# A branch-free tail for the last four experts, one width for the large product, fixed buffers, and logits as column tiles

## The chip, the cores and the metric

The kernel runs on one core of a Trainium2 chip. The metric is the device time of one execution in microseconds, and shorter is better. The core has five engines with a queue of instructions each, which run beside one another and wait for one another by semaphores: PE (matrix products, with PEld as its loading of the stationary operand), DVE and ACT (element-wise work), POOL (element-wise work, and here the indirect transfers) and SP (which only issues transfers). PE writes its results into eight banks of accumulation memory.

## The reference

Three stages follow one another. Block-causal attention gives 1152 token vectors of 512 numbers. A gated product `(x @ w_a) * (x @ w_b) @ w_out` with 1536 inner columns follows (its weights are 64-bit floats). Then each token goes to one of 8 experts:

```python
logits = x @ w_gate                       # 1152 x 8
expert_idx = np.argmax(logits, axis=1)
gate_w = softmax(logits)[np.arange(N), expert_idx]
for i in range(N):                        # capacity = 288 rows per expert
    e = expert_idx[i]
    if counts[e] < capacity:
        disp[e, counts[e]] = x[i]
        pos[i] = counts[e]; counts[e] += 1; keep[i] = True
h = np.maximum(np.einsum('ecd,edf->ecf', disp, w1), 0.0)   # 512 -> 1024
y = np.einsum('ecf,efd->ecd', h, w2)                       # 1024 -> 512
out[i] = gate_w[i] * y[expert_idx[i], pos[i]] if keep[i] else 0
```

How many tokens an expert gets is known only on the chip. With the data drawn here the eight experts get 0, 217, 640 (cut to 288), 274, 3, 2, 2 and 14 tokens.

## The kernel before

**Attention and gated product.** A hand-written order of steps interleaves attention, the decoding of the 64-bit weights, and the first products. Products that must be exact are made of three passes of a faster number format: each operand is split into a high and a low part (`hi`, `lo`), and PE runs hi by hi, hi by lo and lo by hi. This part is untouched but for the buffer of `w_gate`.

**Token stage.** For each of the nine tiles of 128 tokens, PE makes the second product of the gated stage (`y_part`, 36 matmuls, L567). Between pieces of it the steps of the tile before are placed: `y_turn` transposes its 512 columns, `logits` (L589) multiplies with `w_gate`, giving 8 rows by 128 tokens summed over four slices `kd` in one accumulation, ACT copies them, `choose` (L596) transposes them back and DVE finds the maximum and the expert, and `place` (L619) counts positions by a product with a triangle and scatters each token's row into the buffer `xdisp` in device memory by an indirect transfer of POOL (L637). After the last tile the counts of all experts (`cnt`) are known.

**Experts.** The counts are loaded into registers of all five engines (`load_count`, L710). An expert with more than 64 tokens takes the large path: `wide` (L822) computes the first product of all its rows in eight pieces `f`, 12 matmuls each, for 256 or for 288 rows (two forms behind one branch); `blocks` (L854) computes the second product in blocks of 128, 128 and 32 rows, each followed by `put`, an indirect transfer of the rows to the output (L797). An expert with 1 to 64 tokens takes the small path: `few_first` (L878) multiplies 64 rows with the plain 32-bit weights, in two halves that share one bank, with two weight chunks on two halves of PE's columns; `few_turn` transposes, `few_second` (L896) is the second product. An expert with none does nothing. Ahead of each expert's second product stands the preparation of the next one: `x_turn` transposes its rows on PE (L781, three blocks, each in a bank of its own out of a pool of three) and splits them into hi and lo on ACT and DVE (L784, L785), and `split_first` splits its first weights (L744 on ACT, L745 on DVE: two chunks in four pieces). The second weights are split inside `wide`, one piece at every other `f`.

Every one of these is inside a branch on a register that PE, ACT, DVE and POOL take together:

```python
with most(e, HB) as big:
    ...
    x_turn(e + 1)
    split_first(e + 1)
    blocks(e, 0)
with big.Else():
    with least(e) as some:
        few_first(e)
```

The weights come from device memory in chunks of 1 MB (`wraw`, four to an expert, L548), into a pool of nine buffers. Nine are asked for at the start of the token stage, and after each expert SP asks for the next four, as buffers come free. The rows of an expert are read back from `xdisp` by `xload` (L732 to L736).

Of the kernel before, what the change touches and what calls it, by code (L numbers as in the profile page):

```python
# [11 lines left out]
F32 = mybir.dt.float32  # L12
# [14 lines left out]
G = 32  # L27
# [39 lines left out]
def fused_kernel(ctx: ExitStack, tc, q, k, v, w_a, w_b, w_out, w_gate, w1, w2, consts, out, cap):  # L67
# [376 lines left out]
    wg_sb = gp.tile([P, KD, E], F32, name="wg_sb")  # L444
    nc.sync.dma_start(out=wg_sb, in_=w_gate.rearrange("(k p) e -> p k e", p=P))
# [85 lines left out]
    NW = 9  # L531
    wr_pool = es_r.enter_context(tc.tile_pool(name="wr_pool", bufs=NW, side="right"))
# [3 lines left out]
    chunks = [(e, w, c) for e in range(E) for w, n_ in ((0, CPE), (1, KC)) for c in range(n_)]  # L536
    raws = {}

    def fetch_to(m):

        for n in range(len(raws), min(m, len(chunks))):
            e, which, c = chunks[n]
            raw = wr_pool.tile([P, KD, HALF], F32, tag="wraw", name=f"wraw{n}")
# [7 lines left out]
    fetch_to(NW)  # L551
# [33 lines left out]
    def logits(t):  # L585
        s = tok[t]
        plt_ = psG.tile([P, P], F32, tag="plt", name=f"plt{t}")
        for kd in range(KD):
            nc.tensor.matmul(plt_[:E], lhsT=wg_sb[:, kd], rhs=s["yT"][:, kd], start=(kd == 0), stop=(kd == KD - 1))  # L589
        s["lgT"] = sp.tile([E, P], F32, tag="lgT", name=f"lgT{t}")  # L590
        nc.scalar.copy(s["lgT"], plt_[:E])

    def choose(t):
        s = tok[t]
        plg = psG.tile([P, E], F32, tag="plg", name=f"plg{t}")
        nc.tensor.transpose(plg, s["lgT"], ident[:E, :E])  # L596
# [16 lines left out]
        s["oh"] = oh  # L613

    def place(t):
# [4 lines left out]
        nc.tensor.matmul(ppos, lhsT=ones, rhs=acc, start=False, stop=True)  # L620
        t2 = sp.tile([P, E], F32, tag="t2", name=f"t2{t}")
        nc.vector.tensor_tensor(out=t2, in0=ppos, in1=oh, op=ALU.mult)
        nc.vector.tensor_reduce(out=pos, in_=t2, op=ALU.add, axis=AX.X)
        slot = sp.tile([P, 2], F32, tag="slot", name=f"slot{t}")
        nc.vector.tensor_scalar(
            out=slot[:, 0:1], in0=pos, scalar1=float(cap), scalar2=float(FAR), op0=ALU.is_ge, op1=ALU.mult
        )
        nc.vector.scalar_tensor_tensor(
            out=slot[:, 1:2], in0=idx, scalar=float(cap), in1=pos, op0=ALU.mult, op1=ALU.add
        )  # L630
        sl_i = sp.tile([P, 1], I32, tag="sl", name=f"sl{t}")
        nc.vector.tensor_tensor(out=sl_i, in0=slot[:, 0:1], in1=slot[:, 1:2], op=ALU.add)
        nc.vector.tensor_tensor(out=acc, in0=acc, in1=oh, op=ALU.add)
        row = s["row"]
        nc.vector.tensor_scalar_add(sm, sm, 1e-9)
        nc.vector.reciprocal(row[:, DM:DM + 1], sm)
# [6 lines left out]
    for t in range(NT):  # L643
# [24 lines left out]
    few = keep.tile([P, E], F32, name="few")  # L668
    nc.vector.tensor_scalar(out=few, in0=pct, scalar1=float(P // 2), scalar2=-2.0, op0=ALU.is_le, op1=ALU.mult)
# [8 lines left out]
    psH = es_m.enter_context(tc.tile_pool(name="psH", bufs=3, space=PSUM))  # L678
    psT = es_m.enter_context(tc.tile_pool(name="psT", bufs=3, space=PSUM))
    psO = es_m.enter_context(tc.tile_pool(name="psO", bufs=2, space=PSUM))  # L680
# [18 lines left out]
    y_ = [[mp.tile([P, DM], F32, name=f"y{i}_{j}") for j in range(len(blks))] for i in range(2)]  # L699
# [6 lines left out]
    def load_count(e):  # L706
# [7 lines left out]
        hs = [h for g in engines[:4] for h in regs[e, g].val.handles]  # L714
        regs[e] = RuntimeValue.of_register_unchecked(RegisterHandles(hs))
# [9 lines left out]
    def xload(e):  # L725
        if e >= E:
            return
        st[e] = {"xd": []}
        for j, (r, m) in enumerate(blks):
            st[e]["xd"].append(mp.tile([P, ROW], F32, tag=f"xd{j}", name=f"xd{e}_{j}", bufs=3))  # L730
        xd = st[e]["xd"]
        nc.sync.dma_start(out=xd[0][:HB, :], in_=xdisp[e * cap:e * cap + HB, :])  # L732
        with most((e, ET.SP), HB):
            nc.sync.dma_start(out=xd[0][HB:P, :], in_=xdisp[e * cap + HB:e * cap + P, :])
            for j, (r, m) in enumerate(blks[1:], 1):
                nc.sync.dma_start(out=xd[j][:m, :], in_=xdisp[e * cap + r:e * cap + r + m, :])  # L736
# [240 lines left out]
```

## Time and profile before

| | |
|---|---|
| median of three runs | 531.5 us (527.62, 531.5, 532.93) |
| the profiled execution, own time | 535.47 us |
| its span, first to last instruction | 533.4 us |
| mean granted TensorE clock | 0.957 |
| PE busy | 477.7 us, 90% of the span |
| DVE, ACT, POOL busy | 48%, 35%, 24% |
| weight chunks `wraw` | 32 transfers of 1 MB, 10.6 us each from issue to landing (median) |

The profile is one execution. Its own time is 2.1 us over its span, and 4.0 us over the median of the runs. PE's busy time counts pipelined matmuls to their modelled ends, so it says where PE works, not that it works at its peak. [...]

### The profile page before, as it was taken

The numbers are of one execution on the slowest core, as the hardware profiler recorded it, in microseconds if no ns is written. First come the engines' busy times: TensorE is split into PE (matmuls) and PEld (weight loads), VectorE is DVE, ScalarE is ACT, GpSimd is POOL, SyncE is SP. The second block draws the span as 40 slices with busy tenths as digits, with TensorE's granted clock in tenths as the row PEclk, the third lists the DMA queues.
The fourth block names the chain that finished last, engine by engine and source line by source line (L and its number), as shares of the span: only waits on it lengthen the run. The fifth ranks groups of instructions, "written<-read, shape, count | busy, mean of one in ns | idle before, by whom it ended". The sixth has DMA issues, their size and how long they took to land. (4 is left out here: it accounts for less than half of the span.)

```text
span 533.4 us, 7946 instructions
## 1 busy us (share of the span) xinstructions
PE 477.7 (90%) x2808; PEld 379.3 (71%) x2808; DVE 255.1 (48%) x495; ACT 189.0 (35%) x391; POOL 126.8 (24%) x133
## 2 busy tenths in 40 slices
PE   6899999999999899999999999981898999966684
PEld 3465556779999899999977777761887968732241
DVE  2689996736464656473333343434472816010111
ACT  2577777523232324331422222213362615110111
POOL 1447767510413142330102010011101020011010
PEclk9899999999999999999999999996698999896979
DMA  7666310025455565650099010002846327079620
GB/s 166 150 188 173 85 23 2 1 81 179 161 178 177 171 209 180 211 177 1 1 349 378 22 41 20 21 4 68 265 147 237 126 93 280 23 268 328 217 106 4
DMA packets 67260, 73.48 MB, mean 138 GB/s; under 512 B 31395, under 2 KB 43811, under 8 KB 67185
## 3 DMA queue, kind: packets, MB, share of 16 engines
q1 hardware_dynamic: 64384, 68.80, 39.9%
q0 software_dynamic: 1456, 3.29, 1.6%
q8 instruction: 40, 0.66, 0.5%
q10 hardware_dynamic: 1344, 0.44, 0.3%
q14 instruction: 36, 0.29, 0.2%
HBM read 62.12 MB, written 11.72 MB: 138 GB/s over the span
## 5 line engine op out<-in xcount | busy, mean ns | idle before, releaser
L418 PE MATMUL p<-xTh,hi 128*128 128x384 f32 x272 | 91.4, 336 | 3.8 <-ACT asb L483 2.5
L418 PE MATMUL p<-xTh,lo 128*128 128x384 f32 x272 | 90.9, 334 | 0.0
L418 PE MATMUL p<-xTl,hi 128*128 128x384 f32 x272 | 90.9, 334 | 0.0
L278 POOL TENSOR_TENSOR PB<-PB,rs 128x576 f32<-128x576 f32 (+4 forms) x40 | 52.4, 1333 | 42.4 <-DVE rs L267 34.4
L418 PEld LDWEIGHTS p<-xTh,hi 128*128 128x128 f32 x272 | 51.0, 188 | 5.4 <-ACT asb L483 3.9
L418 PEld LDWEIGHTS p<-xTl,hi 128*128 128x128 f32 x272 | 51.1, 188 | 0.0
L418 PEld LDWEIGHTS p<-xTh,lo 128*128 128x128 f32 x272 | 51.1, 188 | 0.0
L822 PE MATMUL ph<-xt,whi 128*128 128x288 f32 (+1 forms) x192 | 41.5, 312 | 4.8 <-DMA xdisp<-row,sl 1.8
L567 PE MATMUL py<-woh,gh 128*128 128x512 f32 x108 | 45.7, 423 | 0.0
L567 PE MATMUL py<-woh,gl 128*128 128x512 f32 x108 | 42.7, 396 | 0.0
L567 PE MATMUL py<-wol,gh 128*128 128x512 f32 x108 | 42.5, 394 | 0.0
L797 POOL DMA_INDIRECT out<-y,ti x12 | 11.3, 945 | 120.1 <-ACT y L861 67.5
L253 ACT ACTIVATE PB<-sc,nm 128x256 f32<-128x256 f32 (+3 forms) x64 | 33.1, 531 | 16.8 <-DVE nm L242 11.4
L211 PE MATMUL sc<-k,q 64*64 64x288 f32 (+4 forms) x192 | 36.8, 493 | 2.2 <-ACT PB L258 1.1
L854 PE MATMUL po<-whi,ht 128*128 128x512 f32 (+1 forms) x112 | 37.9, 407 | 0.4 <-issue 0.4
L822 PEld LDWEIGHTS ph<-xt,whi 128*128 128x128 f32 x192 | 33.4, 207 | 5.5 <-issue 3.6
L381 POOL TENSOR_TENSOR wol<-wob,woh 128x1024 fp32r<-128x1024 f32 x6 | 14.5, 2422 | 92.4 <-ACT woh L380 78.8
L242 DVE TENSOR_REDUCE nm<-sc 128x2 f32<-128x512 f32 (+4 forms) x40 | 31.2, 802 | 8.4 <-PE sc L211 4.2
L408 POOL TENSOR_TENSOR lo<-bits,hi 128x1024 fp32r<-128x1024 f32 x12 | 28.7, 2391 | 24.7 <-ACT hi L402 24.7
L745 DVE TENSOR_TENSOR wlo<-wraw,whi 128x1024 fp32r<-128x1024 f32 x24 | 28.6, 1220 | 9.8 <-ACT whi L744 9.3
L878 PE MATMUL pf<-wraw,xs 128*64 128x256 f32 x128 | 19.7, 458 | 14.8 <-issue 7.5
L484 DVE TENSOR_TENSOR g_sb<-asb,p 128x384 f32<-128x384 f32 x34 | 18.3, 551 | 29.8 <-PE p L418 15.2
(129 smaller groups left out, 809.6 us busy)
## 6 DMA issues: line engine op xcount, KB each, us to landing
wraw<-in_moe_w SPq DMA_DIRECT2D x32, 1024.0 KB, 10.6
raw<-in_moe_w_a SPq DMA_DIRECT2D x12, 512.0 KB, 3.9
raw<-in_moe_w_b SPq DMA_DIRECT2D x12, 512.0 KB, 5.7
wor<-in_moe_w_out SPq DMA_DIRECT2D x6, 1024.0 KB, 6.7
xdisp<-zrow SPq DMA_DIRECT2D x6, 774.0 KB, 8.0
out<-zrow SPq DMA_DIRECT2D x3, 768.0 KB, 7.6
QK<-in_q SPq DMA_DIRECT2D x16, 128.0 KB, 2.9
V<-in_v SPq DMA_DIRECT2D x16, 128.0 KB, 2.6
```

The lines of the kernel that those rows point to most:

```text
L211: nc.tensor.matmul(dst, lhsT=qT[n][hs, P * i:min(P * i + P, S)], rhs=kT[n][hs, c0:c0 + cw], start=True, stop=(i == LAST), skip_group_check ...
L242: nc.vector.tensor_reduce(out=soft[n][0][:, c:c + cnt], in_=view, op=ALU.max, axis=AX.X if i < NQ else AX.XY, negate=True)
L253: nc.scalar.activation(out=dst[:, h], in_=view[:, h], func=AF.Exp, bias=nm[:, c + h:c + h + 1], accum_out=sm[:, c + h:c + h + 1],)
L278: nc.gpsimd.tensor_tensor(out=x, in0=x, in1=r, op=ALU.mult)
L408: nc.gpsimd.tensor_tensor(out=lo, in0=f32(m), in1=f32(hi), op=ALU.subtract)
L418: nc.tensor.matmul(ps, lhsT=lt, rhs=rt, start=(n_ == 0), stop=(n_ == len(seq) - 1))
L484: nc.vector.tensor_tensor(out=g_sb[:, f, c * CH:(c + 1) * CH], in0=asb, in1=pb, op=ALU.mult)
L567: nc.tensor.matmul(s["py"], lhsT=lt[:, f], rhs=rt[:, f], start=(f == 0 and i == 0), stop=(f == NF - 1 and i == 2))
L745: nc.vector.tensor_tensor(out=lo[:, a:a + 2], in0=raw[:, a:a + 2], in1=f32(hi[:, a:a + 2]), op=ALU.subtract)
L822: nc.tensor.matmul(ph[:, 0:n].rearrange("p (g c) -> p g c", c=G), lhsT=lt, rhs=rt, start=(n_ == 0), stop=(n_ == len(seq) - 1),)
L854: nc.tensor.matmul(po[:2 * m if tail else m], lhsT=lt, rhs=rt, start=(f == 0 and i == 0), stop=(f == KF2 - 1 and i == len(seq) - 1),)
L878: nc.tensor.matmul(ph[c * HB:(c + 1) * HB, cs], lhsT=s["xs"][:, kd], rhs=raws[e, 0, c][:, kd, cs], start=(kd == 0), stop=(kd == KD - 1), s ...
```

## The change

- **Tail.** DVE also computes `left`, the largest count of experts 4 to 7. After the first four experts all five engines load it and branch once: if it is over 64, experts 4 to 7 run as before, otherwise `run_few` runs the small path for all four with no further branch. In the small path the two halves of the first product use two banks, and consecutive experts use different ones.
- **One form.** `wide` always computes 288 rows.
- **Buffers.** Pools give way to fixed tiles: twelve weight chunks in place of nine (three are in room that is free only after the token stage), three pairs of hi and lo rooms in place of four, two sets of row buffers `xd` in place of three, one set of output rows `y` in place of two, four banks `pH` for the first product in place of three, two banks `pT` for transposes in place of three. With three rooms `split_first` splits one chunk (two pieces), and `wide` splits the other three, one piece after each of `f` 0 to 5. `split_first` now stands ahead of `x_turn`, and only ACT and DVE take its branch.
- **Start of the experts.** The rows of experts 0 and 1 are read in full without a branch, then chunks 9 to 11; the rows of expert 2 are read after expert 0.
- **Token stage.** `w_gate` is padded with zeros to 32 columns. Each of the four slices `kd` is a matmul of its own on its own 32 columns of PE, the full 128 by 128 result is transposed, and DVE adds the four parts. In `place` one of the DVE steps goes, two stand earlier, and the reciprocal is ahead of the slot.

```diff
-        for kd in range(KD):
-            nc.tensor.matmul(plt_[:E], lhsT=wg_sb[:, kd], rhs=s["yT"][:, kd], start=(kd == 0), stop=(kd == KD - 1))
+            nc.tensor.matmul(
+                plt_[kd * CT:(kd + 1) * CT], lhsT=wg_sb[:, kd], rhs=s["yT"][:, kd], start=True, stop=True,
+                skip_group_check=True, tile_position=(0, kd * CT),
+            )
...
-        nc.tensor.transpose(plg, s["lgT"], ident[:E, :E])
+        nc.tensor.transpose(pl4, s["lgT"], ident)
+        plg = sp.tile([P, E], F32, tag="lg", name=f"lg{t}")
+        nc.vector.tensor_reduce(
+            out=plg, in_=pl4.rearrange("p (k c) -> p c k", c=CT)[:, 0:E], op=ALU.add, axis=AX.X
+        )
...
+    nc.vector.tensor_reduce(out=left, in_=pct[:, E // 2:], op=ALU.max, axis=AX.X)
...
-    parts = {
-        (w, c): [hp.tile([P, KD, HALF], F32R, name=f"w{nm}{w}_{c}") for nm in ("hi", "lo")]
-        for w in range(2) for c in range(CPE)
-    }
+    rooms = [[hp.tile([P, KD, HALF], F32R, name=f"w{nm}{i}") for nm in ("hi", "lo")] for i in range(3)]
+
+    def parts(e, which, c):
+        return rooms[((2 * e + which) * CPE + c) % 3]
...
+    pH = [psM.tile([P, HALF], F32, name=f"pH{i}") for i in range(4)]
+    pT = [psM.tile([P, KD, P], F32, name=f"pT{i}") for i in range(2)]
+    pO = [psM.tile([P, DM], F32, name=f"pO{i}") for i in range(2)]
...
+    def xload_now(es):
...
+        for js in ((0,), range(1, len(blks))):
+            for e in es:
+                for j in js:
+                    r, m = blks[j]
+                    nc.sync.dma_start(out=xd_[e % 2][j][:m, :], in_=xdisp[e * cap + r:e * cap + r + m, :])
...
     def split_first(e):
         if e < E:
-            with most(e, HB):
-                for piece in halves(e, 0):
+            with most((e, "split"), HB):
+                for piece in halves(e, 0, 0):
                     piece()
...
+    def x_all(e):
+        s = st[e]
+        xd, xt = s["xd"], s["xt"]
+        for j, (r, m) in enumerate(blks):
+            pt = pT[j % 2]
+            for kd in range(KD):
+                nc.tensor.transpose(pt[:, kd, :m], xd[j][:m, kd * P:(kd + 1) * P], ident[:m, :m])
...
+            nc.scalar.copy(xh, src)
+            nc.vector.tensor_tensor(out=xl, in0=src, in1=f32(xh), op=ALU.subtract)
...
-        todo = halves(e, 1)
+        todo = halves(e, 0, 1) + halves(e, 1, 0) + halves(e, 1, 1)
...
-            if todo and f % 2 == 0:
+            if todo:
                 todo.pop(0)()
...
     def few_first(e):
-        ph = psH.tile([P, HALF], F32, tag="ph", name=f"pf{e}")
         for g in range(2):
+            ph = pH[e % 2 * 2 + g]
...
-            x_turn(e + 1)
             split_first(e + 1)
+            x_turn(e + 1)
             blocks(e, 0)
...
+    def run_few(e0):
+
+        for e in range(e0, E):
+            few_first(e)
+            few_turn(e, 0)
+            if e + 1 < E:
+                x_rooms(e + 1)
+                x_few(e + 1)
+            few_turn(e, 1)
+            few_second(e)
+            if e + 3 < E:
+                xload(e + 3, whole=False)
+            fetch_to(NW + 2 * CPE * (e + 1))
...
+    run(0, MID)
...
+    with tc.If(regs["left"] > HB) as many:
+        run(MID, E)
+    with many.Else():
...
+        run_few(MID)
```

The change moves instructions at three places. The first is PE at the end of expert 1's first product (`ph` before, `pH` now), where the rows of expert 2 are transposed; `px2_0` to `px2_2` are the three banks before, `pT0` and `pT1` the two banks now, and the waits of a row stand in brackets. Before:

```order
L822 MATMUL ph1_7_256_4343<-xt_3369,wlo0_1_3364 128x256
L908 UNCONDITIONAL_BRANCH
L777 COMPARE_AND_BRANCH
L781 MATMUL px2_0_4359<-cst_62,xd2_0_3454 128x128 [waits DMAHW3_49,DMAHW2_49]
L781 MATMUL px2_0_4359<-cst_62,xd2_0_3454 128x128 x3
L781 MATMUL px2_1_4368<-cst_62,xd2_1_3455 128x128 [waits DMAHW4_49]
L781 MATMUL px2_1_4368<-cst_62,xd2_1_3455 128x128 x3
L781 MATMUL px2_2_4377<-cst_62,xd2_2_3456 128x32 [waits DMAHW5_49]
L781 MATMUL px2_2_4377<-cst_62,xd2_2_3456 128x32 x3
L777 UNCONDITIONAL_BRANCH
```

Now:

```order
L865 MATMUL pH3_3424<-xt_3397,wlo2_3396 128x288
L784 UNCONDITIONAL_BRANCH
L828 COMPARE_AND_BRANCH
L809 MATMUL pT0_3425<-cst_62,xd0_0_3412 128x128 [waits DMAHW4_49,DMAHW3_49,DMAHW2_49]
L809 MATMUL pT0_3425<-cst_62,xd0_0_3412 128x128 x3
L809 MATMUL pT1_3426<-cst_62,xd0_1_3413 128x128 [waits DMAHW5_49]
L809 MATMUL pT1_3426<-cst_62,xd0_1_3413 128x128 x3
L809 MATMUL pT0_3425<-cst_62,xd0_2_3414 128x32 [waits DMAHW6_49,DVE_49]
L809 MATMUL pT0_3425<-cst_62,xd0_2_3414 128x32 x3
L828 UNCONDITIONAL_BRANCH
```

The third transpose now goes into the bank of the first one, and waits for DVE, which reads that bank; before it waited for its transfer alone.

The second place is DVE's queue at the same point, after the last piece of expert 1's first product. `xt` are the low parts of expert 2's rows, `wlo` the low parts of its first weights. Before:

```order
L777 COMPARE_AND_BRANCH
L785 TENSOR_TENSOR xt_3369<-px2_0_4359,xt_3369 128x4x4x32 [waits Activation_49]
L785 TENSOR_TENSOR xt_3369<-px2_1_4368,xt_3369 128x4x4x32 [waits Activation_49]
L785 TENSOR_TENSOR xt_3369<-px2_2_4377,xt_3369 128x4x32 [waits Activation_49]
L777 UNCONDITIONAL_BRANCH
L788 COMPARE_AND_BRANCH
L788 UNCONDITIONAL_BRANCH [waits DVE_49] x2
L753 COMPARE_AND_BRANCH
L745 TENSOR_TENSOR wlo0_0_3362<-wraw8_2542,whi0_0_3361 128x1024 [waits DMAHW1_49,Activation_49]
L745 TENSOR_TENSOR wlo0_0_3362<-wraw8_2542,whi0_0_3361 128x1024 [waits Activation_49]
L745 TENSOR_TENSOR wlo0_1_3364<-wraw9_4069,whi0_1_3363 128x1024 [waits DMAHW2_49,Activation_49]
L745 TENSOR_TENSOR wlo0_1_3364<-wraw9_4069,whi0_1_3363 128x1024 [waits Activation_49]
```

Now:

```order
L784 COMPARE_AND_BRANCH
L776 TENSOR_TENSOR wlo2_3396<-wraw8_2535,whi2_3395 128x1024 [waits DMAHW1_49,DVE_49,Activation_49]
L776 TENSOR_TENSOR wlo2_3396<-wraw8_2535,whi2_3395 128x1024 [waits DVE_49,Activation_49]
L784 UNCONDITIONAL_BRANCH
L784 UNCONDITIONAL_BRANCH [waits DVE_49]
L828 COMPARE_AND_BRANCH
L813 TENSOR_TENSOR xt_3397<-pT0_3425,xt_3397 128x4x4x32 [waits DVE_49,Activation_49]
L813 TENSOR_TENSOR xt_3397<-pT1_3426,xt_3397 128x4x4x32 [waits DVE_49,Activation_49]
L813 TENSOR_TENSOR xt_3397<-pT0_3425,xt_3397 128x4x32 [waits Activation_49]
L828 UNCONDITIONAL_BRANCH
```

The two weight pieces now stand ahead of the three row pieces, of which the first frees the bank that PE waits for; before, four weight pieces stood behind them. ACT's queue, which makes the high parts, has the same new order.

The third place is PE after the second product of expert 4 (`pq4` before, `pO0` now). Before:

```order
L896 MATMUL pq4_6257<-wraw18_5205,hf_3392 64x512
L896 MATMUL pq4_6257<-wraw19_5207,hf_3392 64x512
L753 COMPARE_AND_BRANCH
L753 UNCONDITIONAL_BRANCH x2
L753 COMPARE_AND_BRANCH
L753 UNCONDITIONAL_BRANCH x2
L777 COMPARE_AND_BRANCH
```

Now:

```order
L939 MATMUL pO0_3427<-wraw6_2533,hf_3431 64x512 [waits DVE_49]
L939 MATMUL pO0_3427<-wraw7_2534,hf_3431 64x512
L939 MATMUL pO0_3427<-wraw6_2533,hf_3431 64x512
L939 MATMUL pO0_3427<-wraw7_2534,hf_3431 64x512
L921 MATMUL pH2_3423<-wraw8_2535,xs1_3399 64x256 [waits DMAHW3_49,Activation_49]
L921 MATMUL pH2_3423<-wraw9_3388,xs1_3399 64x256 [waits DMASW4_49,DMASW5_49,DMASW3_49,DMASW6_49,DMASW2_49,DMASW7_49,DMASW1_49,DMAHW4_49,DMASW0_49,Pool_49]
```

Behind the second product there were branches over the other paths, the first part of expert 5 some 240 rows further on; now expert 5's first product (`pH2`) is the next row.

## Rows read from the trace of the kernel before

**Rows 1.** Windows by stage: PE, PEld, DVE, ACT, POOL busy, granted clock, DMA, GB/s

```profile
265.00:358.00 93.00, 92.87 (x448) 69.01 (x446) 34.96 (x121) 20.71 (x40) 10.15 (x15) 1.00 0.32 120
...
403.80:436.50 32.70, 30.89 (x172) 26.74 (x172) 14.64 (x27) 14.12 (x22) 3.95 (x10) 0.95 0.45 157
...
469.70:533.40 63.70, 40.74 (x220) 18.75 (x220) 7.10 (x13) 7.59 (x16) 5.99 (x14) 0.86 0.54 189
```

**Rows 2.** Timeline of PE, one token tile: start, duration, instruction, shape, count

```profile
340.19 0.39 PE L567 MATMUL py<-wol,gh 128*128 128x512 f32 x1
340.42 0.40 PE L567 MATMUL py<-woh,gl 128*128 128x512 f32 x1
340.75 1.04 PE L589 MATMUL plt<-yT,wg_sb 128*8 128x128 f32 x8
341.72 0.50 PE L567 MATMUL py<-woh,gh 128*128 128x512 f32 x1
...
344.01 0.22 PE L596 MATMUL plg<-cst,lgT 8*128 8x8 f32 x1
```

**Rows 3.** Timeline between token stage and first expert; idle time before in brackets

```profile
365.25 0.98 POOL L637 DMA_INDIRECT xdisp<-row,sl  x1 [4.91 <-DVE cnt L670]
...
369.16 0.87 SPq L734 DMA_DIRECT2D xd<-xdisp  x1
...
372.77 2.55 PE L781 MATMUL px<-cst,xd 128*128 128x128 f32 x12 [8.48 <-DVE wlo L745]
...
376.62 0.76 PE L822 MATMUL ph<-xt,whi 128*128 128x256 f32 x2 [1.29 <-POOL gate L773]
```

**Rows 4.** Chain of waits: expert 3's first product

```profile
438.09 13.03 PE ph L822 x95
```

**Rows 5.** Expert 2 to 3: chain of waits, then timelines of ACT and DVE

```profile
420.24 1.23 PE px L781 x12
...
420.76 1.24 ACT L784 CAST xt<-px 128x512 fp32r<-128x512 f32 x3
421.88 3.91 ACT L744 CAST whi<-wraw 128x1024 fp32r<-128x1024 f32 x4
...
421.67 1.47 DVE L785 TENSOR_TENSOR xt<-px,xt 128x512 fp32r<-128x512 f32 x3
423.06 4.62 DVE L745 TENSOR_TENSOR wlo<-wraw,whi 128x1024 fp32r<-128x1024 f32 x4
```

**Rows 6.** Windows of 3 us: granted clock after idle time, transfer rate

```profile
406.00:409.00 3.00, 3.00 (x15) 3.00 (x15) 0.00 (x0) 0.38 (x2) 0.30 (x2) 0.51 0.95 345
...
478.00:481.00 3.00, 2.61 (x14) 1.02 (x16) 0.42 (x1) 0.34 (x1) 0.00 (x0) 1.00 1.05 390
...
484.00:487.00 3.00, 0.20 (x2) 0.23 (x4) 0.00 (x0) 0.00 (x0) 0.94 (x1) 0.59 0.98 328
...
490.00:493.00 3.00, 2.32 (x14) 1.07 (x12) 0.00 (x0) 0.38 (x1) 0.47 (x3) 0.50 1.05 386
```

**Rows 7.** Timeline of the last four experts: PE, SP and POOL

```profile
469.71 2.38 SPq L548 DMA_DIRECT2D wraw<-in_moe_w  x4
...
471.76 1.95 PE L878 MATMUL pf<-wraw,xs 128*64 128x256 f32 x16 [2.12 <-DVE y L807]
...
486.80 3.68 PE L878 MATMUL pf<-wraw,xs 128*64 128x256 f32 x16 [4.39 <-issue]
...
507.26 2.57 PE L878 MATMUL pf<-wraw,xs 128*64 128x256 f32 x16 [3.15 <-issue]
...
518.39 1.95 PE L878 MATMUL pf<-wraw,xs 128*64 128x256 f32 x16 [1.03 <-ACTq L753]
...
521.02 1.95 PE L878 MATMUL pf<-wraw,xs 128*64 128x256 f32 x16 [0.68 <-ACT hr L882]
...
524.00 3.65 PE L896 MATMUL pq<-wraw,hf 128*64 128x512 f32 x16
...
529.49 0.90 POOL L797 DMA_INDIRECT out<-y,ti  x1 [9.38 <-DVE y L807]
```

More of the change, by code (lines that the diff above doesn't have):

```diff
@@ L536, in fused_kernel @@
     chunks = [(e, w, c) for e in range(E) for w, n_ in ((0, CPE), (1, KC)) for c in range(n_)]
+    rawt = [wr_pool.tile([P, KD, HALF], F32, name=f"wraw{i}") for i in range(NW1)]
     raws = {}
@@ L613, in choose @@
         s["oh"] = oh
+        s["first"] = sp.tile([P, 1], F32, tag="first", name=f"first{t}")
+        nc.vector.tensor_scalar(out=s["first"], in0=idx, scalar1=float(cap), scalar2=None, op0=ALU.mult)
+        nc.vector.tensor_scalar_add(sm, sm, 1e-9)
     def place(t):
@@ L620, in place @@
         nc.tensor.matmul(ppos, lhsT=ones, rhs=acc, start=False, stop=True)
+        nc.vector.reciprocal(s["row"][:, DM:DM + 1], sm)
         t2 = sp.tile([P, E], F32, tag="t2", name=f"t2{t}")
@@ L841, in block @@
         r, m = blks[j]
-        po = psO.tile([P, DM], F32, tag="po", name=f"po{e}_{j}")
-        ws = [[w[:, f % KD] for w in parts[1, f // KD]] for f in range(KF2)]
+        po = pO[j % 2]
+        ws = [[w[:, f % KD] for w in parts(e, 1, f // KD)] for f in range(KF2)]
         tail = TAIL and j == len(blks) - 1
@@ L892, in few_second @@
         s = st[e]
[L893 removed]
+        po = pO[e % 2]
         for j in range(KD):
@@ L927, in expert, with run @@
                 x_turn(e + 1)
+    def run(e0, e1):
+        for e in range(e0, e1):
+            load_count(e + 3)
+            expert(e)
+            if e == 0:
+                xload(2)
+            xload(e + 3)
+            fetch_to(NW + 2 * CPE * (e + 1))
[10 more added lines that the diff above has]
+                xload(e + 3, whole=False)
+            fetch_to(NW + 2 * CPE * (e + 1))
     for e in range(3):
         load_count(e)
-    for e in range(3):
-        xload(e)
+    xload_now((0, 1))
+    fetch_to(NW)
     split_first(0)
     x_rooms(0)
-    x_turn(0)
-    for e in range(E):
-        load_count(e + 3)
-        expert(e)
-        xload(e + 3)
-        fetch_to(NW + 2 * CPE * (e + 1))
+    run(0, MID)
+    for g in engines:
+        regs["left", g] = nc.values_load(
+            left[0:1, 0:1], engines=[g], skip_runtime_bounds_check_because="a count of tokens",
+        )
+    regs["left"] = RuntimeValue.of_register_unchecked(
+        RegisterHandles([h for g in engines for h in regs["left", g].val.handles])
+    )
+    have = dict(raws)
+    with tc.If(regs["left"] > HB) as many:
+        run(MID, E)
+    with many.Else():
+        raws.clear()
+        raws.update(have)
+        run_few(MID)
     es_m.close()
```

148 lines of the change are left out of this document (76 added, 72 removed).

## The prediction

> **What bounds the kernel now.** I read the windows by stage first. In the token stage PE is busy 92.87 of 93 us: whatever PE saves there comes off the end. In the stretch of expert 2 it is busy 30.89 of 32.70 us, but in the last 63.7 us, the four small experts, only 40.74, at a mean granted clock of 0.86 [rows 1]. PE's order sets the time everywhere, and in the tail its idle time does, so every term below is PE's time, or what PE waits for. Within 1% of 531.5 us, that is 5.3 us, a measurement of this kernel (its three runs lie 5.3 us apart) does not tell a change from none.
>
> **Token stage, logits.** A tile's eight records of `plt` last 1.04 us, and the matmuls around them start 1.30 us apart (340.42 to 341.72) where neighbours start 0.23 apart (340.19 to 340.42), so the step costs PE about 1.07 us a tile [rows 2]. Now four column groups share the array. What that gives is seen at the small experts: two groups, 16 records of 256 columns, take 1.95 us [rows 7]; at the rate of `plt` (8 x 128 columns in 1.04) they would take 4.2, so two groups halve the time. There the two records of a product stand side by side and the groups alternate; here each group comes once, and only its second record can meet the first of the next. I take five steps for eight, 0.65 us: 0.35 saved (bounds 0, and 0.78 if all four run together). The transpose back was 0.22 us for 8 columns [rows 2]; it gets 128 columns but loses the switch to an 8-row shape: 0.1 saved, bounds -0.2 and +0.3. DVE's added sum lies beside PE's 36 products; only if DVE came a whole group of nine products late (2.1 us) would PE wait for it. Eight tiles stand in the stream (the ninth is below): 8 x 0.45 = **-3.6 us**, bounds +1.6 and -8.6.
> [...] No row of before shows more than two groups.
>
> **From the last token to the first large expert.** Ahead of the last scatter (365.25) the shorter logits, the earlier reciprocal and one DVE step less are worth about 0.9 us, against 0.2 for the added sum. Expert 1's first block came in two transfers, the second issued at 369.16, behind expert 0's and two branches of SP; PE starts its transposes at 372.77 and the product at 376.62 [rows 3]. Now it is one transfer, second in the queue, about 1.5 us sooner; against it 0.6 MB of unneeded rows of expert 0 go partly ahead of expert 1's last block, some 2 us at 345 GB/s [rows 6]. Taken: **-1.5 us**, bounds -3.5 and +1.5. The three chunks behind these rows find their buffers free. SP is held there only for them, and the rows of expert 2, queued behind, are not needed before its transposes.
>
> **One form.** Only expert 1 (217 tokens) used 256 columns. 96 matmuls of 288 take 13.03 us [rows 4], so 32 columns more are 13.03 x 32/288 = 1.45 us; part of it runs at the lower clock: **+1.6 us**.
>
> **Three rooms, two transpose banks.** This is where the change costs. Let T be the end of a large expert's first product, 420.24 for expert 2. Before, twelve transposes followed, then the second product at T+1.23 [rows 5]. Now the third block's transposes wait until DVE has read the first block, and DVE does two weight pieces first. From the rows [rows 5]: ACT starts at T+0.5 and makes two pieces of 0.98 (3.91/4), DVE the low parts of 1.16 each (4.62/4) from T+1.6 to T+3.9, then the first row piece, about 0.7 (half of 1.47), to T+4.65; PE is released at T+4.75 and reaches the second product at T+4.95. That is 3.7 us more, for experts 1 and 2 (expert 3 prepares a small one, in a bank of its own): **+7.4 us**, bounds +5 and +9. Inside the product two pieces more than before lie beside PE, at 1.16 us of DVE in a step of 1.63 (13.03/8); the fourth bank takes a lag, so nothing is added.
> The stall also leaves PE idle for some 4 us. [...] Half speed for 3 to 4 us of dense work loses 1.5 to 2: **+3.4 us** for both, bounds 0 and +8.
>
> **The tail.** Before, the four small experts start at 471.76, the last one at 518.39, and the last product ends at 524.00 + 3.65 = 527.65: 55.9 us [rows 7]. The last one shows the pure work: 9.26 us from 518.39. Its second half (521.02) waited for ACT because both halves share a bank; with two banks it starts 0.9 sooner, and the four transposes of the next expert's rows fill part of the wait for the copies, so I add 0.3: 8.7 us an expert, 34.8 for four. That is 21.1 us less. Do the weights keep up? Chunks 24 to 27 are asked for when expert 3 ends, as in the row of 469.71; four chunks are 4.2 MB, at 390 GB/s [rows 6] 10.8 us; they are needed 17 us into the tail. The last four go out 4.6 to 8.7 us into it, land by 22, and are needed at 26. The one output buffer is written again some 8.7 us after its transfer was issued; the last one of before, issued at 529.49, was over within 3.9 us. What remains is the jump into the new code: PE's idle 4.39 (486.80) and 3.15 us (507.26) have no releaser, and stand while transfers are dense [rows 7]. One such idle may come behind the single branch, 2.5 us between 0 and 4.4 + 3.15. The tail gives **-18.6 us**, bounds -21.5 and -12.
> [...]
>
> **Sum.** -3.6 - 1.5 + 1.6 + 7.4 + 3.4 - 18.6 = -11.3 us. The profiled execution, 535.47 us (span 533.4), would become 524.2. It is 4.0 us over the median, and the median 531.5 becomes **520 us**.
>
> **Rivals.** *The stalls cost less:* the clock stays up and half of the wait for DVE hides, with the tail at its full 21.1: -3.6 - 1.5 + 1.6 + 4 - 21 = -20.5, 511 us. For it: the jump into the first small expert, 2.12 us idle, was followed by a clock of 1.00 at 478 [rows 6, 7]. Against: the queue order of DVE is plain. *The tail keeps half its idle time:* if the idle of 4.39 and 3.15 us comes from the transfers' density and not from the branches, straight code meets it as well, and the tail gives about -8: 531 us. For it: 507.26 stands in the middle of straight code. *Slower:* PE stays at the lower clock after each stall for the whole second product, as it did at expert 5, where 490 to 493 still reads 0.50 [rows 6]. The products of experts 1 and 2 last 11 and 15 us at full clock; at half they cost 26 more in place of 3.4, so 531.5 - 11.3 + 22.6 = 543 us. It decides from about 11 us of low clock per stall beyond the 3 to 4 assumed; the stretch of expert 2, with 406 to 409 at 0.51, averages 0.95 [rows 1], so dense products brought the clock back soon, which speaks against it. *The branch is not taken as meant:* the four small experts all ran the small path (four times two `pf` groups), so no count is over 64; 1%.
>
> **How the numbers follow.** Forecast 50%, small stalls 22%, idle tail 20%, slower 5%, the rest 3%. Faster by over 1%: nearly all of the first two and a third of the third, 0.75; within 1%: 0.18; slower: 0.07. The range 509 to 532 us takes in the first three cases and leaves out the slow one and the far bounds of the token stage.
>
> **What would show it.** In the profile after: `plt` at some 0.65 us a tile and nine tiles some 4 us shorter; between the end of the first product of experts 1 and 2 and their second product about 5 us with PE idle in front of the third transpose, released by DVE; a granted clock near 0.5 just behind; the four small experts 8 to 9 us apart with PE near 90% busy. I would be wrong if the small experts still stood 12 us or more apart, or if the third transpose came right behind the second.

## The result and the profile after

The changed kernel takes 513.63 us (median of four runs, 512.36 to 514.79), the kernel before in the same series 532.21 (527.62 to 535.42). The ratio is 0.9657, 95% interval 0.958 to 0.9733: 18.6 us faster. The forecast was 520 us, the range 509 to 532. The profiled execution takes 514.79 us with a span of 513.0, 20.4 us less than the profiled one of before; its sum was to fall by 11.3.

The windows by stage of the changed kernel, as in [rows 1], for the token stage, the stretch of expert 2 and the tail (us, busy time of PE, PEld, DVE, ACT, POOL, then the granted clock, which is the share of its full speed that the profile says PE was given, DMA share, GB/s):

```profile
267.20:352.30 85.10, 85.09 (x445) 64.72 (x444) 36.99 (x130) 21.05 (x40) 8.61 (x15) 1.00 0.36 131
407.20:442.70 35.50, 31.09 (x173) 26.37 (x173) 14.59 (x28) 14.08 (x22) 5.76 (x10) 0.95 0.41 143
472.10:513.00 40.90, 32.72 (x220) 16.36 (x220) 7.10 (x13) 7.60 (x16) 5.99 (x14) 0.97 0.62 217
```

The token stage is still PE alone, and 7.4 us shorter. Expert 2 is longer than before. The tail has the same 220 matmul records, in 32.7 us of busy time for 40.7, at a clock of 0.97 for 0.86, and 8.2 us of idle time for 23.0.

PE's timeline in one token tile (start, duration, instruction, shape, count), against [rows 2]:

```profile
346.21 0.39 PE L571 MATMUL py<-woh,gl 128*128 128x512 f32 x1
346.53 0.42 PE L593 MATMUL plt<-yT,wg_sb 128*32 128x128 f32 x8
346.89 0.50 PE L571 MATMUL py<-woh,gh 128*128 128x512 f32 x1
...
348.84 0.39 PE L571 MATMUL py<-woh,gl 128*128 128x512 f32 x1
349.07 0.27 PE L603 MATMUL plg<-cst,lgT 128*128 128x128 f32 x1
349.10 0.47 PE L571 MATMUL py<-woh,gh 128*128 128x512 f32 x1
```

The matmuls around `plt` start 0.68 us apart, before 1.30. The transpose back, now of 128 columns, stands between two that start 0.26 us apart, where neighbours start 0.23 apart: it costs next to nothing. Before, the two around the transpose of [rows 2] started 0.48 us apart:

```profile
343.68 0.40 PE L567 MATMUL py<-woh,gl 128*128 128x512 f32 x1
...
344.16 0.50 PE L567 MATMUL py<-woh,gh 128*128 128x512 f32 x1
```

From the last scatter to the first large product, all engines that matter, as in [rows 3]:

```profile
358.94 0.98 POOL L649 DMA_INDIRECT xdisp<-row,sl  x1 [4.59 <-DVE cnt L684]
...
365.45 1.08 PE L809 MATMUL pT<-cst,xd 128*128 128x128 f32 x4 [7.07 <-DMA xd<-xdisp]
...
367.38 0.18 PEld L809 LDWEIGHTS pT<-cst,xd 128*128 128x128 f32 x1 [1.25 <-DMA xd<-xdisp]
...
368.78 1.57 PE L809 MATMUL pT<-cst,xd 128*128 128x128 f32 x8 [2.24 <-issue]
...
370.70 0.61 PE L865 MATMUL pH<-xt,whi 128*128 128x288 f32 x1 [0.35 <-ACT xt L812]
```

The first block comes 1 us sooner after the scatter than before (6.5 us for 7.5), but PE stands idle again in front of the second. The rows account for it until 367.38, when PE loads the first piece of the second block; for the 1.4 us from there to 368.78 the profile names no releaser. The product starts 11.8 us after the scatter; before it was 11.4.

The end of expert 1's first product (386.84), all engines, where [rows 5] shows the like for expert 2:

```profile
386.84 1.04 PE L809 MATMUL pT<-cst,xd 128*128 128x128 f32 x8
...
387.34 1.98 ACT L775 CAST whi<-wraw 128x1024 fp32r<-128x1024 f32 x2
...
388.41 2.36 DVE L776 TENSOR_TENSOR wlo<-wraw,whi 128x1024 fp32r<-128x1024 f32 x2 [0.41 <-ACT whi L775]
389.22 1.07 ACT L812 CAST xt<-pT 128x512 fp32r<-128x512 f32 x2
390.69 1.28 DVE L813 TENSOR_TENSOR xt<-pT,xt 128x512 fp32r<-128x512 f32 x2
391.43 0.63 PE L809 MATMUL pT<-cst,xd 32*128 32x32 f32 x4 [3.56 <-DVE xt L813]
...
391.99 0.80 PE L897 MATMUL pO<-whi,ht 128*128 128x512 f32 x1
```

Read it downwards: two pieces of weights on ACT, their low parts on DVE, then the rows, then PE. The second product starts 5.15 us after the first ended, before 1.33. Behind it the clock is down, at 0.50 until 397 and at 1.00 from 398, as the windows of 3 us (to be read beside [rows 6]) show:

```profile
391.00:394.00 3.00, 2.57 (x9) 2.12 (x10) 1.26 (x3) 0.27 (x1) 0.00 (x0) 0.50 0.72 261
...
397.00:400.00 3.00, 3.00 (x13) 2.40 (x12) 0.00 (x0) 0.00 (x0) 0.00 (x0) 0.88 0.00 0
```

And the first products of the small experts on PE's timeline, which answer to [rows 7]:

```profile
472.90 3.67 PE L921 MATMUL pH<-wraw,xs 128*64 128x256 f32 x32 [0.88 <-SPq L754]
...
481.61 3.62 PE L921 MATMUL pH<-wraw,xs 128*64 128x256 f32 x32
...
490.03 3.62 PE L921 MATMUL pH<-wraw,xs 128*64 128x256 f32 x32
...
498.46 3.62 PE L921 MATMUL pH<-wraw,xs 128*64 128x256 f32 x32
```

They stand 8.4 to 8.7 us apart and start without any wait but the first. The transfers are as dense as they were where PE stood idle before; the window from 482 to 486:

```profile
482.00:486.00 4.00, 3.99 (x36) 2.39 (x32) 1.11 (x2) 1.35 (x3) 0.94 (x1) 1.00 1.06 390
```

**Where the 20.4 us went**, from the starts of PE's groups in both traces (before, after, difference):

| stretch | before | after | us |
|---|---|---|---|
| start to the first `py` | 265.43 | 267.21 | +1.8 |
| token stage, to the end of the last `py` | 92.4 | 85.1 | -7.4 |
| to the first large product | 18.75 | 18.41 | -0.3 |
| expert 1's first product | 14.37 | 16.14 | +1.8 |
| first to second product, experts 1 and 2 | 1.33 each | 5.15, 4.99 | +7.5 |
| their second products, to the end or to expert 3 | 11.46, 15.95 | 14.07, 17.50 | +4.2 |
| gaps ahead of expert 2, of expert 3's second product and of the tail, and low clock behind them | | | -6.4 |
| tail, to the end of the span | 61.6 | 40.1 | -21.5 |

The first line is no effect that a run shows: in ten traces (before, after, experiments 1 to 8) the first `py` starts between 263.6 and 267.6 us, and in two of the same code up to there (before and experiment 2) at 265.4 and 263.6.

### The profile page after: what moved, and what is told of

The parts are those of the page before. It is cut to its first block, busy times and chain, and to the rows that moved or that the text cites. A ratio compares the mean times of both kernels' runs of the same rounds, so it can differ in the third digit from the quotient of the medians.

```text
span 513.0 us, 7684 instructions
## 1 busy us (share of the span) xinstructions
PE 466.8 (91%) x2808; PEld 376.8 (73%) x2808; DVE 257.8 (50%) x513; ACT 189.6 (37%) x391; POOL 127.4 (25%) x134
## 5 line engine op out<-in xcount | busy, mean ns | idle before, releaser
L865 PE MATMUL pH<-xt,whi 128*128 128x288 f32 x192 | 42.1, 313 | 2.8 <-ACTq L910 1.2
L897 PE MATMUL pO<-whi,ht 128*128 128x512 f32 (+1 forms) x112 | 40.1, 428 | 0.0
L865 PEld LDWEIGHTS pH<-xt,whi 128*128 128x128 f32 x192 | 33.1, 201 | 4.4 <-ACTq L910 1.6
L839 POOL DMA_INDIRECT out<-y,ti x12 | 11.4, 946 | 87.9 <-ACT y L904 62.7
L309 PE MATMUL pT<-cst,PB 128*128 128x128 f32 x200 | 29.9, 285 | 0.6 <-POOL PB L278 0.6
## 6 DMA issues: line engine op xcount, KB each, us to landing
wraw<-in_moe_w SPq DMA_DIRECT2D x32, 1024.0 KB, 11.4
```

The lines of the kernel that those rows point to most:

```text
L309: nc.tensor.transpose(pt[:, j * P:(j + 1) * P], tile_at(n, i, kt, h), ident)
L865: nc.tensor.matmul(ph[:, 0:n].rearrange("p (g c) -> p g c", c=G), lhsT=lt, rhs=rt, start=(n_ == 0), stop=(n_ == len(seq) - 1),)
L897: nc.tensor.matmul(po[:2 * m if tail else m], lhsT=lt, rhs=rt, start=(f == 0 and i == 0), stop=(f == KF2 - 1 and i == len(seq) - 1),)
```

## Experiments

The theory: the tail was slow because the engines jump over the other paths' code ahead of each small expert, while weights are moving; the gain is straight code, and the two banks for transposes give part of it back, by a stall and by the low clock behind it. The rivals: the three further chunk buffers made the gain; the idle time comes from dense transfers alone; the stall costs nothing beside other work.

What an experiment gives against the changed kernel is the difference of the medians of two series of runs. The kernel before reads 531.45 to 533.4 us in the experiments' series and 532.21 in the changed kernel's own, so such a difference is good to some 1.6 us; by the ratios it comes out up to that much otherwise.

**1. Branches put back into the tail**

```diff
-    with tc.If(regs["left"] > HB) as many:
-        run(MID, E)
-    with many.Else():
...
-        run_few(MID)
+    run(MID, E)
```

> The changed kernel, but experts 4 to 7 always go through the branching path; twelve chunks, two banks and everything else stay. Theory (the branches made the idle time of the tail): the tail from the first small expert to the end of the span goes from 40.1 back to 55 to 62 us, with idle times of 2 to 4 us on PE ahead of each small expert, and the kernel takes 528 to 536 us. Rival (the three further chunk buffers made the gain): the tail stays within 3 us of 40.1, 513 to 517 us. Half and half would read 520 to 526 us.

527.03 us, ratio to the kernel before 0.9912 (0.9878 to 0.9945): 13.4 us of the gain are gone. From the first small expert (470.54) to the end of the span it is 54.6 us. The first products of experts 5 and 6 on PE's timeline:

```profile
483.51 6.70 PE L921 MATMUL pH<-wraw,xs 128*64 128x256 f32 x32 [3.81 <-DMA wraw<-in_moe_w]
...
498.85 5.36 PE L921 MATMUL pH<-wraw,xs 128*64 128x256 f32 x32 [2.87 <-DMA wraw<-in_moe_w]
```

The idle time is back with all twelve buffers, so branches make it. The transfer named is the last one that ended; expert 5's own chunks were asked for at 440.61, over 40 us earlier, and expert 6's from 470.73 on, some 25 us earlier, where the run's chunks took 11.1 us to land (median). The first of the two idle times lies in dense transfers (384 GB/s on average from 479.6 to 483.6), the second where they run out (68 GB/s from 495.9 to 499). Same work, 6.70 us for 3.67: the clock is low behind the idle time too (0.50 from 484 to 487). The tail did not quite go back to 61.6, so some 7 us of before had other causes.

**2. The kernel before with a straight tail only**

```diff
-    for e in range(E):
+    for e in range(E // 2):
         load_count(e + 3)
         expert(e)
...
+    for e in range(E // 2, E):
...
+        few_first(e)
+        few_turn(e, 0)
+        if e + 1 < E:
+            x_few(e + 1)
+        few_turn(e, 1)
+        few_second(e)
```

> The kernel before with one part of the change alone: experts 4 to 7 run the small path as straight code on every engine but SP, chosen when the program is built and not by a count, so it would be wrong for larger experts; nine chunks and one bank for both halves stay. Theory: the last four experts stand 9 to 9.5 us apart, the stretch from the first of them to the end goes from 61.6 to 42 to 45 us, and the kernel before gets 17 to 20 us faster, 512 to 515 us, as fast as the whole change. Rival (buffers): experts wait for chunks, 12 us and more apart, 526 to 532 us.

512.31 us, 0.9647 (0.9613 to 0.9681): this part alone gives the whole of the change's gain. PE's timeline in the tail, the first halves only:

```profile
464.90 1.95 PE L878 MATMUL pf<-wraw,xs 128*64 128x256 f32 x16 [0.88 <-issue]
...
474.23 1.90 PE L878 MATMUL pf<-wraw,xs 128*64 128x256 f32 x16
...
492.08 0.59 PE L878 MATMUL pf<-wraw,xs 128*64 128x256 f32 x2
493.21 1.94 PE L878 MATMUL pf<-wraw,xs 128*64 128x256 f32 x14 [0.53 <-DMA wraw<-in_moe_w]
```

8.9 to 9.3 us apart, 43.1 us to the end against 61.6, with nine chunks and one bank. There is no decision in this run: the straight code is fixed when the program is built. The rest of the change is worth 3.0 us in the tail (40.1), and outside it gives and takes about as much.

**3. Nine chunks in the changed kernel**

```diff
-    NW1, NW = 9, 12
+    NW1, NW = 9, 9
```

> The changed kernel with nine chunk buffers in place of twelve, branch-free tail kept. Theory: small experts still 8.5 to 10 us apart, one wait of 1 to 3 us for a chunk at expert 6, 514 to 518 us; three transfers less at the entry may give back up to 1 us there. Rival (buffers): 522 to 530 us, with PE waiting for weight chunks ahead of experts 5 to 7.

519.63 us, 0.9769 (0.9731 to 0.9806): 6 us more, between the two. PE waits for chunks at experts 6 and 7; below, those two products and, from SP's timeline, the transfers behind expert 4:

```profile
492.86 3.67 PE L921 MATMUL pH<-wraw,xs 128*64 128x256 f32 x30 [2.14 <-DMA wraw<-in_moe_w]
...
503.74 3.67 PE L921 MATMUL pH<-wraw,xs 128*64 128x256 f32 x30 [1.78 <-DMA wraw<-in_moe_w]
```

```profile
481.01 0.45 SPq L752 DMA_DIRECT2D xd<-xdisp  x1
481.66 15.57 SPq L552 DMA_DIRECT2D wraw<-in_moe_w  x7
```

Experiment 2 has nine chunks as well and waits 0.53 us. What differs is SP's queue there, where the chunks come next at 469.76:

```profile
466.81 2.02 SPq L732 DMA_DIRECT2D xd<-xdisp  x1
```

The row load ahead of the chunks goes out 1.9 us into the tail there and 8.4 us into it here. The change has two sets of row buffers for three, so the load of expert 7's rows must wait until expert 5's have been read, the last time by POOL, and the chunks wait behind it on SP. So the further buffers pay for a wait that the change itself brought in. That the set of rows is the cause follows from the code and these rows; a kernel with three sets and twelve chunks was not run.

**4. Short branches in the straight tail**

```diff
-            few_first(e)
-            few_turn(e, 0)
+            with tc.If(regs["left"] > -1):
+                few_first(e)
+            with tc.If(regs["left"] > -1):
+                few_turn(e, 0)
...
+                with tc.If(regs["left"] > -1):
+                    x_few(e + 1)
...
+            with tc.If(regs["left"] > -1):
+                few_second(e)
```

> The changed kernel with four branches put into each expert of the straight tail, each over a condition that always holds, so every engine compares and goes straight on and nothing is jumped over. [...]

514.32 us, 0.9677 (0.9648 to 0.9705): 0.7 us more for 15 branches, not to be told from nothing, and no idle time in the tail over 0.88 us. A branch that goes straight on cost nothing here that the runs can tell.

**5. The rows ahead of the weights, two banks**

```diff
             wide(e)
+            x_turn(e + 1)
             split_first(e + 1)
-            x_turn(e + 1)
```

> The changed kernel with the order of the kernel before at the end of a large expert's first product: the transposes of the next rows ahead of the first weight pieces; two banks stay. Theory: the third transpose then waits only for ACT's copy and DVE's subtraction of the first block, some 2 us after the end of the first product, so each of the two stalls shrinks from 3.6 to about 1 us: 5 us back, and 1 to 3 us of low clock with it, 506 to 509 us. Rival (the stall is hidden or the weight pieces come late for the next product): 512 to 515 us.

503.39 us, 0.9435 (0.9384 to 0.9486), 10.2 us below the changed kernel. The third transpose of expert 2's rows:

```profile
387.06 0.43 PE L809 MATMUL pT<-cst,xd 32*128 32x32 f32 x4 [1.02 <-DVE xt L813]
```

It waits 1.02 us for 3.56, and the granted clock is 1.00 from 385 to 406 and from 406 to 429 us, past both places.

**6. A bank of its own for the third block**

```diff
-            pt = pT[j % 2]
+            pt = pT[j] if j < 2 else pH[0].rearrange("p (k c) -> p k c", k=KD)
```

> The changed kernel with the third block of rows transposed into a bank of the first product that is free by then; the weight pieces stay ahead of the rows on ACT and DVE. Theory (the bank is what PE waits for): no idle time in front of the third transpose, the second product begins 1.3 us after the end of the first, both stalls of 3.6 us and the low clock behind them go, 503 to 508 us. Rival (the rows of the second block and the weights hold PE anyway, or the clock falls for another reason): 510 to 515 us.

502.52 us, 0.9427 (0.9373 to 0.948), 11.1 us below the changed kernel. PE's timeline at the place of the stall:

```profile
384.94 1.04 PE L809 MATMUL pT<-cst,xd 128*128 128x128 f32 x8
385.91 0.43 PE L809 MATMUL pH<-cst,xd 32*128 32x32 f32 x4
386.27 0.50 PE L897 MATMUL pO<-whi,ht 128*128 128x512 f32 x1
```

The queues of ACT and DVE are as in the changed kernel, and PE waits for neither there. What PE waited for was the bank together with the order of those queues: experiment 5 keeps the two banks and changes the order, this one does the opposite, and in one series they end 0.9 us apart.

**7. PE kept busy through the stall**

```diff
+            if e > 1 and j == 2:
+                wh = parts(e - 1, 1, 0)[0]
+                for i in range(14):
+                    nc.tensor.matmul(pO[1], lhsT=wh[:, i % KD, 0:P], rhs=wh[:, i % KD], start=True, stop=True)
             for kd in range(KD):
```

> The changed kernel with 14 products of no use (some 3.2 us at full clock) put in front of the third transpose of the rows of experts 2 and 3, in a bank that is free there: the stall stays as long, but PE works through it. Theory (the idle time is what lowers the clock): granted clock near 1.0 behind both stalls, their second products 2.6 and 0.8 us shorter, the kernel 2.5 to 4 us faster, 509.5 to 511.5 us. Rival (the clock is low for another reason, or the products delay PE): 513 to 517 us.

509.41 us, 0.9552 (0.9502 to 0.9602), 4.2 us below the changed kernel. PE's timeline, then the window that answers to the first one of the changed kernel:

```profile
385.89 1.03 PE L813 MATMUL pT<-cst,xd 128*128 128x128 f32 x8
386.69 3.45 PE L811 MATMUL pO<-whi 128*128 128x512 f32 x14
390.49 0.43 PE L813 MATMUL pT<-cst,xd 32*128 32x32 f32 x4 [0.35 <-DVE xt L817]
```

```profile
391.00:394.00 3.00, 3.00 (x14) 2.41 (x15) 0.32 (x2) 0.22 (x1) 0.00 (x0) 1.00 1.04 386
```

The third transpose comes 4.6 us after the first, as in the changed kernel, but the clock is 1.00 where it was 0.50. So the idle time lowers the clock, and of the 11.1 us of experiment 6 some 4.2 are clock and 6.9 (the two are of one series) the wait itself.

**8. The logits of before**

```diff
...
-            nc.tensor.matmul(
-                plt_[kd * CT:(kd + 1) * CT], lhsT=wg_sb[:, kd], rhs=s["yT"][:, kd], start=True, stop=True,
-                skip_group_check=True, tile_position=(0, kd * CT),
-            )
+            nc.tensor.matmul(plt_[:E], lhsT=wg_sb[:, kd], rhs=s["yT"][:, kd], start=(kd == 0), stop=(kd == KD - 1))
...
-        nc.tensor.transpose(pl4, s["lgT"], ident)
+        nc.tensor.transpose(plg, s["lgT"], ident[:E, :E])
```

> The changed kernel with the logits of the kernel before (one product of 8 rows summed over the four slices, a transpose back of 8 columns, no sum on DVE). If all that the token stage gained (7.4 us by the trace, against 3.6 in the forecast) is the column groups: 520 to 522 us, with tiles 0.9 us further apart. If half of it comes from the other edits there (reciprocal and sums moved, DVE steps): 516 to 518 us.

520.47 us, 0.9758 (0.9707 to 0.981): 6.8 us more. POOL's scatters stand 10.46 us apart (six tiles from 295.58 to 358.33), with the column groups 9.59 (295.62 to 353.17), in the kernel before 10.50. The column groups are the token stage's gain; the other edits there are worth 0.04 us a tile.

**9. Long jumps in the straight tail**

```diff
         for e in range(e0, E):
+            with tc.If(regs["left"] > HB):
+                wide(e)
+                for j in range(len(blks)):
+                    block(e, j)
             few_first(e)
```

> The changed kernel with one branch ahead of each small expert, over a large expert's two products, whose condition never holds: every engine jumps over some 180 matmuls that aren't run, and the small experts' code, buffers and transfers stay. [...] Rival (the path of branches costs by its many waits and comparisons, not by the distance): 514 to 517 us, as the run with short branches.

529.01 us, 0.9928 (0.9901 to 0.9955), 15.4 us more than the changed kernel; my estimate, from the idle times of experiment 1 (3.81 and 2.87 us), was 6 to 12. The first products of experts 4 to 6 on PE's timeline:

```profile
476.26 6.11 PE L921 MATMUL pH<-wraw,xs 128*64 128x256 f32 x32 [5.84 <-DMA wraw<-in_moe_w]
...
490.06 5.87 PE L921 MATMUL pH<-wraw,xs 128*64 128x256 f32 x32 [2.72 <-PEq L983]
...
502.65 3.67 PE L921 MATMUL pH<-wraw,xs 128*64 128x256 f32 x32 [1.75 <-DVEq L983]
```

Nothing is run that the changed kernel doesn't run, and the same data is there; only code is jumped over. The first two gaps fall into the transfers (194 GB/s on average from 470 to 476.3, with 377 at its end, and 380 from 487 to 490.2) and last 5.84 and 2.72 us; the first also holds the jump of the single branch, 0.88 us in the changed kernel. The third stands behind the transfers, and so does a fourth: 1.75 and 1.80 us at 9 and 0 GB/s. In the first gap the DMA view of 470 to 476.3 us lists packets of instructions beside those of the weights (queue, packets, MB, share):

```profile
q14 instruction: 4, 0.03, 1.5%
q8 instruction: 1, 0.02, 1.3%
```

**10. Branches, but no weights moving**

```diff
-            nc.sync.dma_start(out=raw, in_=src)
+            if n < 2 * NW:
+                nc.sync.dma_start(out=raw, in_=src)
...
+    run(MID, E)
```

> The changed kernel with experts 4 to 7 on the branching path, and without the transfers of the last eight weight chunks, so that no weights move in the tail: experts 6 and 7 are computed from old contents, which leaves their reading out. [...] Rival (a jump costs the same with or without transfers): tail 52 to 55 us, 525 to 528 us.

518.62 us, 0.9737 (0.969 to 0.9785), 8.4 us below experiment 1. The first products of experts 5 and 6 on PE's timeline:

```profile
481.63 4.24 PE L922 MATMUL pH<-wraw,xs 128*64 128x256 f32 x32 [0.92 <-SPq L755]
...
492.90 3.81 PE L922 MATMUL pH<-wraw,xs 128*64 128x256 f32 x32 [1.25 <-ACT t L849]
```

The same jumps cost 0.9 to 1.3 us, and the clock reads 1.00 throughout. The tail is 46.0 us; 5.9 us more than straight code remain, in these and in the short waits between a small expert's steps. So of the 14.5 us that the branches cost in experiment 1, 8.6 need the transfers; a jump without them costs less, not nothing. What makes a jump dearer under transfers is not shown: a packet of the instruction queue q8 (16 KB) lasts no longer in the gap of experiment 9 under 380 GB/s, 1.1 us, than in the one without, 1.3 us (its share of 16 engines: 2.1% of 3.2 us, 4.2% of 1.9 us).

**11. Own bank and another order of the rows**

```diff
-        for js in ((0,), range(1, len(blks))):
-            for e in es:
-                for j in js:
...
+        for e, js in ((0, (0,)), (1, (0, 1, 2)), (0, (1, 2))):
+            for j in js:
...
```

> The changed kernel with a bank of the first product for the third block of rows (for expert 1 one that is not used first), and the rows read at the entry in another order: expert 0's first block, all of expert 1's, then the rest of expert 0's. Theory: 11 us from the stalls as in the run with an own bank, and 1 to 2.5 us at the entry, where PE waited for expert 1's last blocks behind expert 0's unneeded ones: 500 to 502 us. Rival (the last blocks come no sooner, as latency and not the order holds them): 502 to 503.5 us.

502.13 us, 0.9441 (0.9394 to 0.9487): not to be told from experiment 6. PE's timeline at the entry:

```profile
363.62 1.30 PE L808 MATMUL pT<-cst,xd 128*128 128x128 f32 x5 [7.63 <-DMA xd<-xdisp]
366.42 0.80 PE L808 MATMUL pT<-cst,xd 128*128 128x128 f32 x3 [1.49 <-issue]
```

Five transposes run in one go, the fifth being the first of the second block, so that block's rows are there, where the changed kernel waits for them until 367.38. But then PE stands idle in the middle of the block for nothing that the profile shows. From `pct` to the rest of the second block it is 10.59 us, in the changed kernel 10.57 to its first transpose. The other order brought the rows sooner, and the idle time behind took the gain; what makes it stays open.

**12. The same, with work for PE at the entry**

```diff
+    for i in range(12):
+        nc.tensor.transpose(pO[1][:, 0:P], cst[:, 0:P], ident)
     for e in range(3):
         load_count(e)
...
+            if e == 1:
+                for i in range((6, 4, 0)[j]):
+                    nc.tensor.transpose(pO[1][:, 0:P], cst[:, 0:P], ident)
...
```

> The kernel with the own bank and the rows of expert 1 ahead, and 22 transposes of no use on PE in its idle time between the token stage and the first large product. Theory (the granted clock is 0.50 from 358 to 377 us because PE stands idle, and 6 us of the first product run at half speed): the clock is back sooner, 1 to 3 us less than without them, 498 to 501 us. Rival (some 4 us of light work do not bring the clock back, or they delay PE): the same as without them or up to 1 us more.

505.4 us, 0.9489 (0.9443 to 0.9535): 3.3 us more, a miss. PE's timeline:

```profile
357.80 2.79 PE L997 MATMUL pO<-cst 128*128 128x128 f32 x12 [0.62 <-DVE cnt L684]
...
367.74 1.53 PE L809 MATMUL pO<-cst 128*128 128x128 f32 x6 [7.15 <-issue]
```

The clock stayed at 0.50 until 376, and PE, which now takes its branch to expert 1 when transfers have begun (127 GB/s from 360 to 362), stands 7.15 us for nothing that the profile shows; in experiment 11 its first transpose of rows stands at 363.62. Transfers run at 236 to 370 GB/s from 362 to 368; what holds PE there is not shown.

## Why the prediction was right, and where its terms were off

The likeliest case came true, 6 us faster than forecast. By its own steps, in the order of its sum (the differences are those of the table above):

- *Logits, -3.6:* **mis-sized**; the runs say -7.4 by the trace and -6.8 by experiment 8. I took five steps for eight, 0.65 us a tile, from the two groups of the small experts [rows 7]; the step now stretches the stream by 0.45 us (0.68 less 0.23). The transpose saved 0.22 us a tile and not 0.1: with 8 columns it had stretched the stream by 0.25 us (0.48 less 0.23), with 128 it stretches it by 0.03. The records of a tile went from 1.04 to 0.42 us, by a factor of 2.5, where the five steps made it 1.6.
- *Entry, -1.5:* -0.3. The transfer of the first block did come sooner, but a second idle time, in front of the second block, took its place: 2.24 us, of them some 0.8 for the rows, queued behind expert 0's, and 1.4 without a releaser. Experiment 11 takes the first away and keeps the second, which the sum had not foreseen.
- *One form, +1.6:* +1.8. The two traces differ in the clock there as well (0.50 for 5.4 us of the product before, from 376.62 to 382, and for 6.3 us after, from 370.70 to 377), so this is agreement and no measurement of the 32 columns.
- *Stalls, +7.4:* +7.5 by the trace, 6.9 by experiments 6 and 7. Bank, queue order and DVE's last piece were read rightly; PE waited 3.56 us both times.
- *Low clock behind them, +3.4:* +4.2 by the trace and by experiment 7. Half speed for 3 to 4 us was an estimate, from windows behind other idle times [rows 6]; no run of before shows it for these stalls. In the changed kernel the clock was 0.50 from 391 to 397 and 0.88 from 397 to 400 behind the first, 0.68 from 424 to 427 and 0.76 from 427 to 430 behind the second. It is not the same in each execution: in the trace of experiment 4, with the same two stalls, the second products of experts 1 and 2 are together 2.9 us longer than in experiment 7's, in those of experiments 1 and 3 4.8 to 5.0.
- *Tail, -18.6:* -21.5, the first bound. The experts stand 8.4 to 8.7 us apart, as worked out; of the 2.5 us that I kept back for one idle time behind the single branch 0.88 came, put down to SP. That the branches cause the idle time was my estimate, from where it stood [rows 7]: experiments 1, 2 and 9 show that the branches, not the buffers, made the tail slow. Experiment 4 puts 15 branches that go straight on at 0.7 us, and 0.9 to 5.8 us of idle time stand at the long jumps (experiments 9 and 10); what an engine waits for at a jump is not shown. Transfers of 390 GB/s run beside the straight code without a gap, so the rival of the idle tail is out, in its pure form; experiment 10 shows that it held half of the truth, since without transfers the tail with branches takes 46.0 us and not 54.6. The row that spoke for that rival, 3.15 us idle ahead of 507.26 in the middle of straight code [rows 7], has no like where the branches are gone (experiment 2); what held PE at that place no run shows.
- *Left out of the sum:* the gaps of before ahead of expert 2, of expert 3's second product and of the tail, and the low clock behind the first two, are shorter or gone, -6.4 us. Part of it is the profiled execution of before and not the change: experiment 2 has before's code up to the tail, an idle time of 1.68 us ahead of expert 2 and a clock of 1.00 behind it, where [rows 6] show 0.51 after 1.82 us. It reaches the tail at 464.90 and before at 471.76, 6.9 us apart, of which 1.2 lie in the gap right ahead of the changed code; so a difference of this size needs no change of the kernel. The medians, 18.6 us apart, hold less of it than the spans.

The rival of small stalls had the time nearly right (511) and the reason wrong: the stalls were full, and the gain was elsewhere. The slow rival is out: the clock was back at 1.00 from 398 behind the first stall and from 430 behind the second, 6 and 5 us after the second products began (391.99 and 425.20). With the bank of experiment 6 the change gives 31 us and not 19 (502.52 against 533.4 in that series).

## What to carry to other kernels

Where several small pieces of work stand one behind the other while weights are fetched, ask first which jumps stand between them: straight code for the four small experts was worth 19 us here (experiment 2; with branches put back into the changed kernel 13 are gone), and 15 short branches in it cost 0.7, less than the runs can tell. When fixed buffers take the place of a pool, go through every buffer that was taken away and ask which queue now stands behind it: two banks for three, with the weights moved ahead of the rows, cost 11 us, and undoing either one gave 10 or 11 back; two row sets for three were, by the rows of experiment 3, paid for with three megabytes of chunk buffers. A stall of PE is to be priced with the low clock behind it, here 2 us (experiment 7: 4.2 for two) on top of 3.6.

## What the runs showed that was not expected

- The same jump cost PE 2.72 us under transfers and 1.8 us without (experiment 9). The branches of a small expert cost 3.81 us under dense transfers and 2.87 us where they ran out (experiment 1), against 0.92 and 1.25 us with none (experiment 10).
- Four groups of 32 columns took 0.42 us for what one after the other took 1.04, and a transpose of 128 columns disturbed the stream of 512-column matmuls less (0.03 us) than one of 8 rows (0.25).
- Gaps that look alike ended differently: 1.82 us idle, then a granted clock of 0.51 (before, expert 2); 1.68 us, then 1.00 (experiment 2); 1.17 us, then 1.00 (after). What decides between them no run here tells.
- In experiment 12 twelve transposes from 357.80 on filled 2.79 us, and the granted clock from 360 to 362 still read 0.50.
